# Block 0's last feed-forward quarter as Strassen products in a retention and squared-ReLU kernel

## The chip, the cores and the metric

The kernel runs on one core of a Trainium2 chip. The metric is the device time of one execution in microseconds, as the median of several runs. The names of the engines are those of the profile: PE does matmuls, PEld is PE's loading of weights, DVE is the vector engine, ACT the scalar engine, POOL GpSimd, and SP the queue from which nearly all DMAs are issued.

## The reference, cut to what matters

```python
q, k, v: (8, 8, 576, 64)          # batch, heads, sequence, head size
scores = scale * np.matmul(q, k.transpose(0, 1, 3, 2))
Dmat = np.where(rel >= 0, gamma[:, None, None] ** rel[None, :, :], 0.0)
ret = np.matmul(scores * Dmat[None], v)
x = ret.transpose(0, 2, 1, 3).reshape(4608, 512)
h = np.maximum(x @ w_in, 0.0)     # w_in: (512, 2048)
out = h * h @ w_out               # w_out: (2048, 512)
```

Retention, a causal attention with decay and no softmax, makes x of 4608 tokens by 512. Two feed-forward products follow, with a squared ReLU between them. The weights come in as 64-bit floats and are turned into 32-bit ones by integer operations on the chip.

## The kernel before

**Tiling.** The 4608 tokens are 36 chunks of 128 (`N_CH`) and nine blocks of 512 (`N_BLK`), four chunks to a block. Retention goes chunk by chunk and leaves x of block n, transposed, in a room of SBUF, `xT[n]`. Two rooms alternate, so block n writes over the x of block n - 2. The first feed-forward product of a block is cut into four quarters by `mp`, of 512 of the 2048 columns. It is stored to DRAM as five combinations (`G_KEPT`) of the squared result. When all nine blocks are done, a last stage from line 1141 on takes these back and does the second product as two nested levels of seven Strassen products, with block 0 as the last of `BLOCKS`.

**Two ways of doing a quarter.** Blocks 1 to 8 use `ffn_in` (line 700): seven products of Strassen's scheme (`PRODUCTS`), each of four matmuls with 256 columns at line 717. A 32-bit matmul shows in the profile as two instructions, so a product shows as eight. The three sums a, b and c lie in three PSUM tiles of one pool of three (`ps_f`). DVE adds and squares the results (lines 729 to 743); the fifth product (j = 4, line 736) is read on DVE from the tile of b, into which the seventh (j = 6) accumulates next. The left sides of the products are sums of weights (`sum_w_in`, lines 257 to 260); the right sides are sums of x (`sum_x`, lines 637 to 640), made on DVE. At the start the weights aren't all there yet. Block 0 therefore uses `first_in` (line 667), sixteen plain steps. A step takes one converted weight piece of 128 columns, does four matmuls of 512 columns (line 677, eight instructions), and lets ACT do ReLU and square (lines 683 and 685). The two sums that block 0's store lacks, S1 and S3, are made by `sums_0` (line 1005) in the last stage: DRAM to SBUF, two DVE sums at line 1020, and back, for each of eight slices.

**Conversion of the weights.** A piece of `w_in` is converted by six parts in order, one per call unit of `convert` (lines 227 to 244). The first two are on DVE; `beside` is on ACT (line 235); then come three more on DVE, of which the first doesn't need ACT's result and the second does. Ending a piece triggers the fetch of a later one. `w_out` is converted in the same way, in small parts placed in blocks 1 to 7 by a rate (`late_w2`), and goes to DRAM.

**What sets the order.** Every engine's instructions stand in the order in which this program writes them; there is no planner. The loop at line 915 visits the chunks. A visit, `whole(i - 1)`, does the chunk's matmuls with 64 by 64 weights, in which ACT copies the running state (`grown`, line 501) and x (`x_out`, line 550) and DVE masks the scores (line 491). Then `ffn(i - 1)` runs some feed-forward steps from the list `steps`: three plain ones in block 0, seven products afterwards, so that a block takes four visits. In block 0 each step is preceded by up to four of ACT's copies (`move`), six parts of conversion, and one of two DVE transposes of a later chunk's q and k (`flip`, line 416). The 16 copies per chunk (line 431) distribute what these transposes made. `loads` issues the q, k and v of chunks two or three ahead on SP; POOL scales q (line 396) and v (line 495) as they land.

A guard in `x_out` (line 546) runs leftover steps before x is written over:

```python
while steps and steps[0][0] <= n - 2:
    step()
```

Of the kernel before, what the change touches and what calls it, by code (L numbers as in the profile page):

```python
# [15 lines left out]
C = 128  # L16
CH = C // 2
TOK = 512
# [23 lines left out]
def kernel(  # L42
# [33 lines left out]
    nc = tc.nc  # L76
# [7 lines left out]
    N_DM = d_model // 128  # L84
    N_DF = d_ff // 128
    N_M = N_DF // 2
    N_MP = N_M // 2
    N_MQ = N_M // 2
    N_BLK = n_tok // TOK
    NP = len(PRODUCTS)  # L90
# [34 lines left out]
    G_KEPT = ("A11", "S1", "A12", "S3", "A22")  # L125
# [3 lines left out]
    room = const.tile([128, 15872], F32, name="room")  # L129
# [34 lines left out]
    pieces = [(0, m, e) for m in range(N_M) for e in range(2)]  # L164
    pieces += [(1, mq + mh * N_MQ, e) for mq in range(N_MQ) for mh in range(2) for e in range(2)]
    N_W1 = N_DF
    N_HALF = 1
    stage = [W[5].rearrange("p (o s f) -> p o s f", o=4, s=NP),
             W[6][:, 0:3 * NP * 128].rearrange("p (o s f) -> p o s f", o=3, s=NP)]
# [136 lines left out]
    n_made = [0]  # L306
# [26 lines left out]
    def convert(count):  # L333
        for _ in range(count):
            f = next(w_in_steps, None)
            f and f()
# [32 lines left out]

    st = {i: {} for i in range(N_CH)}  # L370
    u_ps = [None]
    xT = {n: xT_room[1 - n % 2] for n in range(N_BLK)}

# [265 lines left out]

    sums = {}

    def g_of(mp):
        return {name: g_room[mp % 2][:, s, :, :] for s, name in enumerate(G_KEPT)}

    def g_store(n, mp, name):
        nc.sync.dma_start(g_dram[n, G_KEPT.index(name), :, 2 * mp:2 * mp + 2, :], g_of(mp)[name])

    def g_sums(n, mp):  # L650

        g = g_of(mp)
        return [
            lambda: [nc.vector.tensor_tensor(g["S1"], g["S3"], g["A22"], op=ALU.add), g_store(n, mp, "A12")],
            lambda: [nc.vector.tensor_tensor(g["S3"], g["A11"], g["S3"], op=ALU.subtract), g_store(n, mp, "S1")],
            lambda: g_store(n, mp, "S3"),
        ]
# [9 lines left out]
    def first_in(j, halves=(0, 1), at=(0, HT)):  # L667

        assert n_made[0] > j
        wi, m, e = pieces[j]  # L670
        mp, mm = divmod(m, 2)
        p = ps_f.tile([128, 2, HT], F32, tag="f", name="h_ps")
        w = w_in[mp][:, mm, 2 * e:2 * e + 2, :, :].rearrange("p s c f -> p (s c) f")
        lo, hi = halves[0], halves[-1] + 1
        p = p[:, lo:hi, at[0]:at[1]]
        for c in range(N_DM):
            nc.tensor.matmul(p, lhsT=w[:, c, :], rhs=xT[0][:, c, :].rearrange("p (h t) -> p h t", h=2)[:, lo:hi, at[0]:at[1]],  # L677
                             start=(c == 0), stop=(c == N_DM - 1))

        t = g_room[mp % 2][:, 2:5:2, mm, :] if e else g_room[mp % 2][:, 0:4:3, mm, :]  # L680
        t = t[:, lo:hi, at[0]:at[1]]
        some(2)
        nc.scalar.activation(t, p, AF.Relu)
        if hi - lo == 2:
            queue.append(lambda: nc.scalar.activation(t, t, AF.Square))
        else:
            queue.append(lambda: nc.vector.tensor_tensor(t, t, t, op=ALU.mult))
        if mm and e and hi == 2 and at[1] == HT:
            queue.append(lambda: [nc.sync.dma_start(
                g_dram[0, a:b, :, 2 * mp:2 * mp + 2, :].rearrange("s p m t -> p s (m t)"),  # L690
                g_room[mp % 2][:, a:b, :, :].rearrange("p s m t -> p s (m t)")) for a, b in QUARTERS])
        if j >= N_W1 - 4:

            sums_w.setdefault(0, sum_w_in(0)).pop(0)()
            if n_next[0] > 1:
                if 1 not in sums_x:
                    sums_x[1] = sum_x(1)
                sums_x[1].pop(0)()

    def ffn_in(n, mp, j):  # L700

        if j == 0 and mp == 0:

            if n == 1:
                transfers.extend((N_BLK, lambda i=i: fetch_w(i)) for i in range(N_W1, N_W1 + 3))
            if n not in sums_x:
                sums_x[n] = sum_x(n)
            for f in sums_x[n]:
                f()
        left, right, to = PRODUCTS[j]  # L710
        if j in OPENS:
            sums[to] = ps_f.tile([128, 2, HT], F32, tag="f", name=f"h_{to}")
        p = sums[to]
        for mm in range(2):
            w = w_in[mp][:, mm, WI_SLOT[left], :, :]
            for c in range(2):
                nc.tensor.matmul(p[:, mm, :], lhsT=w[:, c, :], rhs=xs[n][right][:, c, :],  # L717
                                 start=(j in OPENS and mm == 0 and c == 0), stop=(j in CLOSES and c == 1),
                                 skip_group_check=True)
        g = g_of(mp)  # L720
        p1, u2, p15 = (p_room[mp % 2][:, s, :, :] for s in range(3))

        def square(t):
            nc.vector.scalar_tensor_tensor(t, t, 0.0, t, op0=ALU.max, op1=ALU.mult)  # L724

        if j == 0:
            nc.scalar.copy(p1, p)
        elif j == 1:
            nc.vector.tensor_tensor(u2, p, p1, op=ALU.add)
        elif j == 2:  # L730
            nc.vector.tensor_tensor(p15, p, p1, op=ALU.add)
        elif j == 3:
            nc.scalar.activation(g["A11"], p, AF.Relu)
        elif j == 4:
            nc.scalar.activation(g["A11"], g["A11"], AF.Square)
            nc.vector.tensor_tensor(g["A22"], p, p15, op=ALU.add)
            square(g["A22"])
        elif j == 5:

            nc.vector.tensor_tensor(g["S3"], p, u2, op=ALU.add)  # L740
            square(g["S3"])
        else:
            nc.vector.tensor_tensor(g["A12"], p, p1, op=ALU.add)
            square(g["A12"])
            queue.extend(g_sums(n, mp))

        if j == 5:
            g_store(n, mp, "A11")
            transfers.append((n, lambda: g_store(n, mp, "A22")))

        if mp == N_MP - 1 and j in (3, 4, 5) and n_next[0] > n + 1:
            if n + 1 not in sums_x:
                sums_x[n + 1] = sum_x(n + 1)
            sums_x[n + 1].pop(0)()
        if j in (6, 0, 1, 2, 3):
            some(2 if n == 1 and mp == 0 else 1)
        if n == 1 and 1 <= j < 5 and mp + 1 < N_MP:
            sums_w.setdefault(mp + 1, sum_w_in(mp + 1)).pop(0)()

        late_w2 = 0.94 * (done[0] - N_0 - 8) - n_w2[0]  # L760
        count = 0 if busy[0] or n == 1 and j == 4 else 2 if late_w2 > 1.5 and j in (0, 3) and n > 1 else late_w2 > 0
        while w_out_next[0] and (count or type(w_out_next[0]) is list):
            f = w_out_next[0]
            if held[0] and type(f) is tuple or ahead[0] <= QUIET and type(f) is list:
                break
            assert n_w2[0] or not [t for t in transfers if t[0] == N_BLK]
            n_w2[0] += 1
            count -= type(f) is not list
            w_out_next[0] = next(w_out_steps, None)
            for f in f if type(f) in (tuple, list) else (f,):  # L770
                f()
            if type(w_out_next[0]) is list:
                break
        if n == N_BLK - 2 and mp == 3 and j in (0, 3):
            assert w_out_next[0] is None
            fetch_w2(j // 3)
# [12 lines left out]
    def block_steps(n):  # L789
        if n == 0:  # L790
            seconds = [(0, first_in, j, (1,), (C, HT)) for j in range(N_HALF)]
            return seconds + [(0, first_in, j) for j in range(N_HALF, N_W1)]
        return [(n, ffn_in, n, mp, j) for mp in range(N_MP) for j in range(NP)]

    QUIET = 2

# [10 lines left out]

    N_0 = N_W1  # L810
    done = [0]

    def ffn(i):

        if steps and steps[0][0] == 0:

            for _ in range((N_W1 - N_EARLY) * C // TOK):
                move(4)
                convert(6)
                for f in flips[:1]:  # L820
                    f()
                del flips[:1]
                step()
            return
        count = N_MP * NP * C // TOK
        while steps and count:
            held[0] = count <= 1

            due = sum(m[0] <= i + 2 for m in moves)
            move(max(2, min(4, -(-due // (count - 1)))) if count > 1 else 0)  # L830
            ahead[0] = count
            busy[0] = len(flips) > 0
            for f in flips[:1]:
                f()
            del flips[:1]
            step()
            count -= 1
        held[0] = busy[0] = False
        ahead[0] = N_DF
# [164 lines left out]

    def sums_0():

        for m in range(N_M):
            t = late1.tile([128, len(G_KEPT), HT], F32, tag="g0", name="g0")

            def move(parts, out):  # L1010
# [213 lines left out]
```

## Time and profile before

| What | us |
|---|---|
| Median of 3 runs | 932.11 (931.95 to 932.25) |
| Profiled execution | 931.9 |
| Its span, first to last instruction | 930.2 |
| First plain step of the last twelve | 43.46 |
| Block 1's first product | 95.12 |
| Last stage, about | 541 to the end |
| DMA over the span | 181.29 MB, mean 195 GB/s |

The profile is of one execution. Times in it count from the first instruction. The span is the time from the first to the last instruction, and the rest of the execution's own time (1.7 us) lies around it. A line of a timeline has the start, the length, the engine, the line of the kernel, the operation and the tiles, and the number of instructions that were merged. A line of waits has the waiting engine and line, then what released it, with the sum in us, the count and the longest. A line of the table by stage has the window, its length, and for PE, PEld, DVE, ACT and POOL the busy time and the number of instructions, then the granted clock, the share of DMA and GB/s.

### The profile page before, as it was taken

What the parts mean: (1) busy time and instruction counts of PE and PEld (TensorE: products, weight loads), DVE (VectorE), ACT (ScalarE), POOL (GpSimd) and SP (SyncE); (2) the same over time, 40 slices, a digit from 0 to 9 for tenths busy, and PEclk for the clock granted to TensorE, in tenths of its full rate; (3) what the DMA queues carried; (4) which work ended last, traced back from release to release, by engine and by line L of the source; (5) the groups of instructions that cost most, each with busy time, mean ns of one, the idle gap of its engine ahead of it and who ended that gap; (6) DMA issues with size and microseconds to landing.
All of it is one profiled execution on the core that took longest, in us unless ns stands there. A gap on an engine that the chain in (4) does not pass through costs nothing.

```text
span 930.2 us, 21072 instructions
## 1 busy us (share of the span) xinstructions
PE 922.4 (99%) x8548; PEld 830.2 (89%) x8548; DVE 755.4 (81%) x1215; ACT 346.2 (37%) x788; POOL 82.9 (9%) x82
## 2 busy tenths in 40 slices
PE   8999999999999999999999999999999999999997
PEld 7654888888888888888888899999999999999997
DVE  5888788888898888979876587888888888877877
ACT  3457767667676676676711110000000000000000
POOL 3222111011111111211000000000000000000000
PEclk9999999999999999999999999999999999999999
DMA  9998657578666775784379996566666575465523
GB/s 226 220 270 218 166 153 202 161 214 267 167 180 184 259 216 146 223 271 137 114 258 355 383 318 193 145 176 191 168 180 183 156 206 155 114 178 142 151 79 68
DMA packets 297376, 181.29 MB, mean 195 GB/s; under 512 B 194368, under 2 KB 270272, under 8 KB 296384
## 3 DMA queue, kind: packets, MB, share of 16 engines
q1 hardware_dynamic: 292208, 178.84, 66.5%
q10 hardware_dynamic: 5072, 1.12, 0.6%
q8 instruction: 67, 1.10, 0.5%
q14 instruction: 29, 0.24, 0.1%
HBM read 109.39 MB, written 70.52 MB: 193 GB/s over the span
## 4 chain that ended last, share of the span: by engine, by line
PE 98%; DVE 1%; DMA 1%; SPq 0%; issue 0%; ACT 0%; DVEq 0%
PE h_b L717 18%; PE o_b L1061 18%; PE h_a L717 12%; PE h_c L717 12%; PE o_c L1061 12%; PE o_a L1061 12%; PE h_ps L677 6%; PE x_ps L574 3%; PE sc_ps L480 2%; PE x_ps L609 1%; PE u_ps L568 1%; DMA q_ld<-in_q_dram 1%; PE sc_ps L509 0%; PE t_ps L445 0%; PE x_ps L535 0%; DVE room L513 0%
## 5 line engine op out<-in xcount | busy, mean ns | idle before, releaser
L717 PE MATMUL h_b<-room,w 128*128 128x256 f32 x768 | 181.4, 379 | 0.0
L431 ACT COPY qk<-flip 32x256 f32<-32x256 f32 x432 | 173.8, 402 | 6.7
L717 PEld LDWEIGHTS h_b<-room,w 128*128 128x128 f32 x768 | 145.9, 190 | 19.8
L717 PE MATMUL h_a<-room,w 128*128 128x256 f32 x512 | 123.9, 385 | 0.0
L717 PE MATMUL h_c<-room,w 128*128 128x256 f32 x512 | 121.0, 379 | 0.0
L717 PEld LDWEIGHTS h_c<-room,w 128*128 128x128 f32 x512 | 97.3, 190 | 13.2
L717 PEld LDWEIGHTS h_a<-room,w 128*128 128x128 f32 x512 | 95.0, 190 | 13.7
L1061 PE MATMUL o_b<-room,w 128*128 128x192 f32 x496 | 90.8, 326 | 0.0
L1074 ACT COPY r<-o_a 128x192 f32<-128x192 f32 x28 | 8.9, 319 | 209.4 <-PE o_a L1061 209.4
L1061 PEld LDWEIGHTS o_b<-room,w 128*128 128x128 f32 x496 | 82.3, 190 | 0.0
L724 DVE SCALAR_TENSOR_TENSOR room<-room 128x512 f32<-128x512 f32 x96 | 66.7, 695 | 3.3
L396 POOL TENSOR_TENSOR q_ld<-q_ld,dv 128x512 f32<-128x512 f32 x34 | 37.7, 1110 | 286.1 <-DMA q_ld<-in_q_dram 257.2
L1061 PE MATMUL o_a<-a,w 128*128 128x192 f32 x352 | 62.6, 326 | 0.0
L1061 PE MATMUL o_c<-room,w 128*128 128x192 f32 x336 | 61.5, 326 | 0.0
L1061 PE MATMUL o_b<-s,w 128*128 128x192 f32 x336 | 61.5, 326 | 0.0
L1061 PE MATMUL o_c<-s,w 128*128 128x192 f32 x336 | 61.5, 326 | 0.0
L677 PE MATMUL h_ps<-room,w 128*128 128x512 f32 (+1 forms) x152 | 57.7, 532 | 0.7 <-DVE w L244 0.6
L1061 PEld LDWEIGHTS o_a<-a,w 128*128 128x128 f32 x352 | 58.1, 190 | 0.1
L1061 PE MATMUL o_a<-room,w 128*128 128x192 f32 x320 | 56.9, 326 | 0.0
L1061 PEld LDWEIGHTS o_c<-room,w 128*128 128x128 f32 x336 | 55.8, 190 | 0.0
L1061 PEld LDWEIGHTS o_b<-s,w 128*128 128x128 f32 x336 | 55.8, 190 | 0.0
L1061 PEld LDWEIGHTS o_c<-s,w 128*128 128x128 f32 x336 | 55.8, 190 | 0.0
(116 smaller groups left out, 1409.2 us busy)
## 6 DMA issues: line engine op xcount, KB each, us to landing
g_dram<-room SPq DMA_DIRECT2D x164, 256.0 KB, 3.8
a<-g_dram SPq DMA_DIRECT2D x30, 512.0 KB, 5.3
room<-g_dram SPq DMA_DIRECT2D x28, 512.0 KB, 5.0
w_dram<-w SPq DMA_DIRECT2D x28, 448.0 KB, 4.5
w<-w_dram SPq DMA_DIRECT2D x7, 1792.0 KB, 9.8
q_ld<-in_q_dram SPq DMA_DIRECT2D x64, 128.0 KB, 4.1
w<-in_moe_w_in_dram SPq DMA_DIRECT2D x16, 512.0 KB, 6.3
w<-in_moe_w_out_dram SPq DMA_DIRECT2D x64, 128.0 KB, 3.4
```

Of the source, the lines that this page charges most:

```text
L396: engine.tensor_tensor(t, t, dv[:, heads, at:at + 1].to_broadcast(list(t.shape)), op=ALU.mult)
L431: nc.scalar.copy(*moves.pop(0)[2:])
L480: nc.tensor.matmul(st[i]["sc"][e][rows(h), hp, :], lhsT=st[i]["kT"][rows(e), hp, t], rhs=st[i]["qT"][rows(e), hp, t], start=True, stop=Tru ...
L568: return [lambda hp=hp, e=e, b=b: nc.tensor.matmul(u[rows(e), hp, :], lhsT=loaded[i][1][rows(h), 2 * hp + e, :], rhs=st[i]["vs"][rows(h), ...
L574: return [lambda hp=hp, e=e, b=b: nc.tensor.matmul(x_at(hp, e, b, h), lhsT=s["vs"][rows(h), head(hp, e), :], rhs=s["ret"][rows(h), e, hp, ...
L609: m = nc.tensor.matmul(x_at(hp, e, b, h), lhsT=u[rows(e), hp, :], rhs=s["qT"][rows(e), hp, CH * h:CH * h + CH], start=clears(b, e), stop=F ...
L677: nc.tensor.matmul(p, lhsT=w[:, c, :], rhs=xT[0][:, c, :].rearrange("p (h t) -> p h t", h=2)[:, lo:hi, at[0]:at[1]], start=(c == 0), stop= ...
L717: nc.tensor.matmul(p[:, mm, :], lhsT=w[:, c, :], rhs=xs[n][right][:, c, :], start=(j in OPENS and mm == 0 and c == 0), stop=(j in CLOSES a ...
L724: nc.vector.scalar_tensor_tensor(t, t, 0.0, t, op0=ALU.max, op1=ALU.mult)
L1061: nc.tensor.matmul(p, lhsT=w_out[j][:, m, WO_SLOT[right], :], rhs=s["lefts"][left][:, m, :], start=(i in OPENS and m == 0), stop=(i in CLO ...
L1074: nc.scalar.copy(r[:, 0, LEFT], p)
```

## The change

Block 0 does only the pieces 0 to 11 as plain steps (`N_PLAIN`), which are its first three quarters. Its last quarter becomes seven products of `ffn_in`, placed after the 28 of block 1 and marked as 2, so that the guard lets them stand until block 4's x is due. Since block 0's x is needed until then, `xT[0]` gets a room of its own, which was unused at that time. The plain steps are dealt out as 1, 2, 2 and 3 to the chunk visits 4 to 7 instead of three each, and both transposes of a chunk are put in the first step. With six parts per step, 14 of 16 pieces are converted in block 0; the parts of the last two are put at fixed places in block 1's first half. The conversion of `w_out` begins seven steps later. The two G rooms alternate by a new rule (`side`), the x sums of block 0 are made before its products and those of block 2 after, and `sums_0` covers six slices instead of eight. The list of steps is longer by seven from block 1 on; as each visit still takes seven, the guard runs seven of them at once in `x_out` of chunk 16.

```diff
+    N_PLAIN = N_W1 - 4
...
-    xT = {n: xT_room[1 - n % 2] for n in range(N_BLK)}
+    xT = {n: xT_room[1 - n % 2] for n in range(1, N_BLK)}
+    xT[0] = room[:, 5120:7168].rearrange("p (c t) -> p c t", c=N_DM)
...
-    def g_of(mp):
-        return {name: g_room[mp % 2][:, s, :, :] for s, name in enumerate(G_KEPT)}
+    def side(n, mp):
+        return (3 + mp if n == 1 else 7 if n == 0 else mp) % 2
+
+    def g_of(n, mp):
+        return {name: g_room[side(n, mp)][:, s, :, :] for s, name in enumerate(G_KEPT)}
...
-        if j >= N_W1 - 4:
+        if j >= N_PLAIN - 4:
...
-        if j == 0 and mp == 0:
+        if j == 0 and (mp == 0 or n == 0):
...
-        if mp == N_MP - 1 and j in (3, 4, 5) and n_next[0] > n + 1:
-            if n + 1 not in sums_x:
-                sums_x[n + 1] = sum_x(n + 1)
-            sums_x[n + 1].pop(0)()
+        after = {1: 0, 0: 2}.get(n, n + 1)
+        if mp == N_MP - 1 and j in (3, 4, 5) and n_next[0] > after:
+            if after not in sums_x:
+                sums_x[after] = sum_x(after)
+            sums_x[after].pop(0)()
...
         if n == 1 and 1 <= j < 5 and mp + 1 < N_MP:
+            assert n_made[0] >= 4 * (mp + 2)
             sums_w.setdefault(mp + 1, sum_w_in(mp + 1)).pop(0)()
-
-        late_w2 = 0.94 * (done[0] - N_0 - 8) - n_w2[0]
+        if n == 1:
+            convert({0: 2, 1: 1, 3: 2, 5: 1}.get(j, 0))
+
+        late_w2 = 0.94 * (done[0] - N_0 - 15) - n_w2[0]
...
-            return seconds + [(0, first_in, j) for j in range(N_HALF, N_W1)]
-        return [(n, ffn_in, n, mp, j) for mp in range(N_MP) for j in range(NP)]
+            return seconds + [(0, first_in, j) for j in range(N_HALF, N_PLAIN)]
+        made_ = [(n, ffn_in, n, mp, j) for mp in range(N_MP) for j in range(NP)]
+        if n == 1:
+            made_ += [(2, ffn_in, 0, N_MP - 1, j) for j in range(NP)]
+        return made_
...
-    N_0 = N_W1
+    N_0 = N_PLAIN
...
-            for _ in range((N_W1 - N_EARLY) * C // TOK):
+            for _ in range({4: 1, 7: 3}.get(i, 2)):
                 move(4)
                 convert(6)
-                for f in flips[:1]:
+                for f in flips:
                     f()
-                del flips[:1]
+                del flips[:]
                 step()
...
-        for m in range(N_M):
+        for m in range(2 * (N_MP - 1)):
             t = late1.tile([128, len(G_KEPT), HT], F32, tag="g0", name="g0")
```

More of the change, by code (lines that the diff above doesn't have):

```diff
@@ L642 @@
     sums = {}
-    def g_of(mp):
-        return {name: g_room[mp % 2][:, s, :, :] for s, name in enumerate(G_KEPT)}
+    def side(n, mp):
+        return (3 + mp if n == 1 else 7 if n == 0 else mp) % 2
+    def g_of(n, mp):
+        return {name: g_room[side(n, mp)][:, s, :, :] for s, name in enumerate(G_KEPT)}
     def g_store(n, mp, name):
-        nc.sync.dma_start(g_dram[n, G_KEPT.index(name), :, 2 * mp:2 * mp + 2, :], g_of(mp)[name])
+        nc.sync.dma_start(g_dram[n, G_KEPT.index(name), :, 2 * mp:2 * mp + 2, :], g_of(n, mp)[name])
     def g_sums(n, mp):
-        g = g_of(mp)
+        g = g_of(n, mp)
         return [
@@ L719, in ffn_in @@
                                  skip_group_check=True)
-        g = g_of(mp)
-        p1, u2, p15 = (p_room[mp % 2][:, s, :, :] for s in range(3))
+        g = g_of(n, mp)
+        p1, u2, p15 = (p_room[side(n, mp)][:, s, :, :] for s in range(3))
         def square(t):
@@ L765, in ffn_in @@
                 break
-            assert n_w2[0] or not [t for t in transfers if t[0] == N_BLK]
+            assert n_made[0] == N_W1 and (n_w2[0] or not [t for t in transfers if t[0] == N_BLK])
             n_w2[0] += 1
```

## The prediction

> **What bounds the kernel now.** I read the page's busy times first, then what PE waited for, then the order of time on PE and DVE around block 0. The page says that the tensor engine is the bound:
>
> ```profile
> span 930.2 us, 21072 instructions
> PE 922.4 (99%) x8548; PEld 830.2 (89%) x8548; DVE 755.4 (81%) x1215; ACT 346.2 (37%) x788; POOL 82.9 (9%) x82
> ```
>
> The share is modelled, so it must be checked against PE's waits. From 15 us to the end there is one:
>
> ```profile
> PE h_ps L677 <- DVE w L244: 0.6, 1, 0.6
> ```
>
> So a microsecond of PE work that goes is a microsecond of time, and any wait that comes is one too. Two views give PE's prices. The timeline of PE in block 1 (start, length, then eight instructions of one product):
>
> ```profile
> 111.31 1.89 PE L717 MATMUL h_b<-room,w 128*128 128x256 f32 x8
> 113.04 1.89 PE L717 MATMUL h_c<-room,w 128*128 128x256 f32 x8
> 114.77 1.89 PE L717 MATMUL h_a<-room,w 128*128 128x256 f32 x8
> ```
>
> From start to start a product takes 1.73 us (113.04 - 111.31); the 1.89 contains an overlap. The timeline of weight loads in a run of three plain steps of block 0 (24 instructions from 43.46):
>
> ```profile
> 44.00 0.19 PEld L677 LDWEIGHTS h_ps<-room,w 128*128 128x128 f32 x1 [0.24 <-issue]
> 53.01 0.19 PEld L677 LDWEIGHTS h_ps<-room,w 128*128 128x128 f32 x1 [0.24 <-issue]
> ```
>
> These are 21 loads apart: 9.01 / 21 = 0.429 us each, so a plain step of eight is 3.43 us, twice a product. Next is the slack of DVE, since the change packs its work closer. The table by stage (PE, PEld, DVE, ACT, POOL busy):
>
> ```profile
> 43.46:95.12 51.66, 51.66 (x628) 27.17 (x624) 43.78 (x69) 33.80 (x67) 12.96 (x11) 1.00 0.94 240
> 95.12:104.06 8.94, 8.94 (x47) 7.90 (x42) 5.76 (x9) 8.35 (x20) 0.31 (x1) 1.00 0.60 153
> ```
>
> The first row is the last twelve plain steps, the second runs from block 1's start to the moment when DVE takes its fifth product (L736 at 104.06). DVE is free for 60.60 - 49.54 = 11.06 us there. Part of that freedom is not for use, as the waits of DVE in the first stretch show:
>
> ```profile
> DVE qk L491 <- PE sc_ps L480: 4.3, 4, 2.1
> DVE w L241 <- ACT w L235: 3.2, 6, 1.1
> ```
>
> The second line is the ping-pong inside a weight conversion: DVE makes the exponent (L227), ACT scales it (L235), DVE needs it again (L241). A conversion on DVE is these five operations, in the groups by line from 44 to 94 us:
>
> ```profile
> L241 DVE SCALAR_TENSOR_TENSOR w<-w,w 128x512 f32<-128x512 f32 x11 | 9.0, 815 | 3.8 <-ACT w L235 3.2
> L238 DVE SCALAR_TENSOR_TENSOR w<-w,w 128x512 f32<-128x512 uint32 x11 | 8.4, 761 | 0.3
> L244 DVE SCALAR_TENSOR_TENSOR w<-w,w 128x512 uint32<-128x512 uint32 x11 | 8.3, 759 | 0.4
> L227 DVE TENSOR_SCALAR w<-w 128x512 uint32<-128x512 uint32 x10 | 4.6, 463 | 0.0
> L231 DVE TENSOR_SCALAR w<-w 128x512 uint32<-128x512 uint32 x10 | 4.2, 420 | 0.0
> ```
>
> Means: 0.815 + 0.761 + 0.759 + 0.463 + 0.420 = 3.22 us a piece.
>
> **What the Trainium skill says.** (1) "Trainium Kernel Development and Optimization", Quick Reference, Reading a trace: matmul busy time is a bad metric of the distance to the limit. This trace agrees in that it shows 99% whether or not PE is well fed, so I use pitches. (2) "PSUM — Partial Sum Buffer", Engine vs sequencer instructions: the queues of ScalarE, VectorE and GpSimdE are strict FIFO, and matmuls start in order. The trace agrees: DVE's conversions, sums and evictions follow the program order, so whatever is queued late delays what stands behind it. (3) "SBUF — State Buffer", Who interferes with whom: a DVE operation with two SBUF inputs and a GpSimd operation that reads SBUF lock each other out. The trace agrees: L238 at 78.11 took 1.44 us instead of 0.69 while a POOL scaling ran from 77.95 to 79.01. The means above contain that.
>
> **The change, part by part.**
>
> PE work. Out go plain steps 12 to 15: 4 x 3.43 = 13.73 us. In come seven products: 7 x 1.726 = 12.08 us (113.04 to 119.95 is four products in 6.91). The number of chunk visits is the same, and the seven that are run at once in `x_out` of chunk 16 adjoin the seven of `ffn(16)`, so no switch is added. Sum: **-1.65 us**.
>
> DVE and ACT work. The four plain steps used ACT for relu and square (0.59 and 0.63 us each, hidden). The products bring eight DVE evictions and squares, two G sums and four x sums, 14 x about 0.61 us (pitch of 736 to 724 and the like) = 8.5 us in a 14.36 us period. Blocks 2 to 8 have the same load in their last quarter and PE keeps its 1.73 pitch there (block 1: 138.21 to 152.5). The two phases after each other, block 1's last quarter and this one, are both of that kind. I cost it at nothing; uncovered, a DVE surplus of 0.5 us at one product.
>
> Late stage. `sums_0` handles 6 slices instead of 8: four fewer of L1020 (0.416 us each) on a DVE that is busy 318.9 of 384 us from 541 to 925, where PE never waits: 0. Fewer SP transfers there, 0. Block 0's last quarter is stored by `g_store` as block 1's is; DMA share is 0.56 around there: 0.
>
> `xT[0]` in its own room: the ACT copy is the same: 0. Block 2's later weight steps (`late_w2` with 15 for 8) begin seven steps later in block 1 and stand where they stood in block 2, since N_0 falls by 4 and seven steps are added: 0.
>
> The packed stretch. This is the cost. PE reaches block 1 earlier by 4 x 3.43 = 13.7 us, and DVE must have done nearly the same work. What DVE no longer has to do before it takes block 1's fifth product: piece 15 (3.22) and the last operation of piece 14 (0.76), together 3.98 us; piece 14's other parts are put by `convert` at j = 0, 1, 3. So DVE has 49.54 - 3.98 = 45.56 us of work in 60.60 - 13.73 = 46.87: 97% full, 1.3 us free where it had 11. What idle time can't be filled: the ACT ping-pong, 3.2 us before and about 2.7 for 9 of 11 pieces; and a wait for the scores at L491, up to 2.0 us in the second chunk (`ffn(5)`: two pieces end about 57, PE brings the scores about 59; it was 2.1 before); together 2.7 to 4.7. DVE then comes 1.4 to 3.4 us late to the fifth product. PE tolerates some of it: the seventh product accumulates into the bank that DVE reads (h_b), one product later: 1.73 - 0.69 - 0.1 = 0.9 us. What is queued behind the late read is j = 5's and j = 6's adds and squares; PE waits for them in turn. Stall: 0.5 to 2.5 us. Lower bound 0, if DVE is late only where PE has slack; a gain is excluded, since PE never waits there now. Upper bound: contention with POOL of 0.75 us hits once or twice more in the packed order, 4 us. ACT has its own form of it: in `ffn(6)` both flips come in the first step, so ACT's chunk copies wait for DVE's transposes, and `grown(7,1)` behind them releases PE's next u matmul; the same for chunk 9's copies before its scores. I get 0 to 1.1 us for each. They don't add: while PE waits early, DVE catches up. I take **+1.5 us** for the whole, the middle of 0.5 and 2.5.
>
> Loads. The stretch is DMA-full (0.94). In each chunk fewer weight fetches precede the next loads, and one G store moves out. v of chunk 7 is scaled by 56.2 (landed 54.9; two fetches, two loads and the like ahead of it are unchanged); PE will need it at 43.46 + 3.6 (one step with its edges) + 2.8 (chunk visit, 53.96 to 56.72) + 7.05 (two steps) + 1.3 (visit's start to its first v of the next chunk, 67.22 to 68.50) = 58.2: slack 2.0 us. Later chunks have 3 us and more. Cost 0; uncovered, 1 to 2 us.
>
> Sum: -1.65 + 1.5 = -0.15. The profiled execution took 931.9 (span 930.2 and 1.7 around it), so 931.75; the median of the runs is 932.11, 0.2 above it: **932.0**.
>
> **The rivals.** *The whole gain*: DVE's and ACT's lateness stays within PE's tolerance. For it: PE is 0.9 us tolerant and the adds before that have two or three products of room. Against: 1.3 us free in 46.9. It gives 932.1 - 1.65 = 930.5. *Slower*: DVE's backlog before block 1, through ACT. The one mechanism: conversions, transposes and ACT's copies in turn make each wait for the other in `ffn(6)` and `ffn(7)`, and DVE is more than 0.9 + 1.65 + 1.9 = 4.4 us late at the fifth product; from 2.5 us late on it is slower than before at all. Price 4 us and more: 932.1 - 1.65 + 4.5 = 935.0. For it: ACT was 9.3 of 10.5 us busy in the last three plain steps, and gets two more conversions there. Against: a stall itself lets DVE catch up. *A load comes late*: chunk 7's v or q, 1 to 2 us besides the 1.5: 933.5. Against it: the loads ahead are fewer. *More than the gain*: nothing in the profile offers PE more than 1.65.
>
> **How the numbers follow.** Forecast 932.0 (931 to 933.2): 0.50. Whole gain 930.5: 0.25. Slower 935.0: 0.15. Late load 933.5: 0.08. Something better: 0.02. A measurement of this kernel can tell about 0.2% from no change, here 1.9 us: 930.2 to 934.0 counts as the same. The whole gain lies just inside it; a fifth of it may fall out (0.05). Faster 0.06, same 0.78, slower 0.16. Range: 930.3 (whole gain) to 934.2, which leaves out most of the slower case.
>
> **What would show it.** Products at a pitch of 1.73 and block 1 starting near 81.4 us (95.12 - 13.7) if nothing waits; PE's waits listing L717 on DVE L736 or room L729, or sc_ps on ACT L431, in sum some 1.5 us; DVE busy about 97% of the stretch from 43 us to block 1's fifth product; the late stage of equal length. Wrong: PE waits of over 3.5 us or none; a wait for POOL v_ld; a pitch over 1.73 in the quarter after block 1 or around chunk 16.

## The result, and the profile after

The changed kernel is slower by 0.4%: 935.6 us as the median of 6 runs (934.55 to 936.2) beside 932.05 us for the kernel before on the same chip (6 runs). The ratio is 1.0038, 95% interval 1.0025 to 1.0051. The profiled execution took 936.2 us, the slowest of the six, with a span of 934.4; before it was 931.9 and 930.2.

The page's first lines, of the kernel after. PE is still the busiest engine at 99%, and the sum of its work as the profile shows it hardly changes, so these lines don't say where 4 us went:

```profile
span 934.4 us, 21125 instructions
PE 922.3 (99%) x8572; PEld 835.3 (89%) x8572; DVE 765.5 (82%) x1225; ACT 343.1 (37%) x783; POOL 82.6 (9%) x82
```

The waits of PE from 15 us on, where the kernel before had one of 0.6 us:

```profile
PE h_b L722 <- DVE room L734: 2.4, 1, 2.4
PE h_ps L682 <- issue: 1.3, 1, 1.3
PE h_b L722 <- DVE room L741: 0.8, 1, 0.8
PE h_ps L682 <- DVE w L245: 0.5, 1, 0.5
PE u_ps L570 <- ACT u_sb L503: 0.5, 1, 0.5
```

L722 is the product matmul (L717 before), L734 the eviction of the second product (L729 before), L741 that of the fifth (L736 before). Block 1's first quarter in the timeline of PE shows the two large ones in their places, before the fifth and the seventh product:

```profile
83.90 1.99 PE L722 MATMUL h_a<-room,w 128*128 128x256 f32 x8
85.73 1.89 PE L722 MATMUL h_b<-room,w 128*128 128x256 f32 x8
87.46 1.89 PE L722 MATMUL h_c<-room,w 128*128 128x256 f32 x8
89.19 1.89 PE L722 MATMUL h_a<-room,w 128*128 128x256 f32 x8
93.45 1.99 PE L722 MATMUL h_b<-room,w 128*128 128x256 f32 x8 [2.38 <-DVE room L734]
95.28 1.89 PE L722 MATMUL h_c<-room,w 128*128 128x256 f32 x8
97.97 1.99 PE L722 MATMUL h_b<-room,w 128*128 128x256 f32 x8 [0.80 <-DVE room L741]
```

Only the packed stretch is longer than it should be. The starts of the runs of weight loads cut it into chunk visits and runs of feed-forward steps; lengths in us:

| | step, then visit of chunk 5 | steps, visit 6 | steps, visit 7 | steps, visit 8 | block 1's first quarter |
|---|---|---|---|---|---|
| lengths that before's runs and visits give | 3.63, 2.77 | 7.06, 2.77 | 7.06, 2.12 | 10.50, 2.01 | 12.28 |
| after | 3.63, 2.77 | 8.60, 3.11 | 7.06, 2.86 | 10.50, 2.03 | 16.00 |

The excess is 1.54 + 0.34 + 0.74 + 0.02 + 3.72 = 6.36 us. PE's listed waits in the stretch make 5.0 of it (2.4 + 1.3 + 0.8 + 0.5; that for L245 lies ahead of it); the rest is lost around them and in gaps too short for the list. From block 1's second quarter to the last stage all is as planned: 445.15 us (101.97 to 547.12) beside 433.07 before (109.48 to 542.55). The difference is 12.08 us, the seven added products to the hundredth. So -13.73 + 12.08 + 6.36 = 4.7. With 0.12 us less before the stretch and 0.37 less in the last stage's end, this is the 4.2 by which the span grew.

The table by stage for that stretch of the kernel after. Its end is where DVE takes the fifth product, as in the prediction's table:

```profile
43.34:83.90 40.56, 38.71 (x596) 21.28 (x593) 32.68 (x53) 25.84 (x55) 10.80 (x10) 1.00 1.00 256
83.90:97.23 13.33, 10.89 (x52) 8.96 (x48) 13.02 (x19) 11.03 (x24) 3.48 (x3) 1.00 1.03 231
```

DVE's work is 32.68 + 13.02 = 45.70 us; 45.56 had been forecast. But it needed 53.89 us for it, not 46.87. Its waits from 43.34 to 97.3:

```profile
DVE w L242 <- ACT w L236: 5.0, 5, 1.8
DVE qk L493 <- PE sc_ps L482: 2.4, 2, 1.9
```

The wait at L493 is 1.95 us in the stretch; the other 0.43 ended just before it. The ping-pong inside the conversions cost 5.0 us for 10 pieces, where it cost 3.2 for 11 before. In the timeline of DVE one sees the four large waits and then the late evictions:

```profile
56.25 0.69 DVE L242 SCALAR_TENSOR_TENSOR w<-w,w 128x512 f32<-128x512 f32 x1 [1.81 <-ACT w L236]
63.32 0.69 DVE L242 SCALAR_TENSOR_TENSOR w<-w,w 128x512 f32<-128x512 f32 x1 [0.88 <-ACT w L236]
69.15 0.69 DVE L242 SCALAR_TENSOR_TENSOR w<-w,w 128x512 f32<-128x512 f32 x1 [0.95 <-ACT w L236]
74.73 0.69 DVE L242 SCALAR_TENSOR_TENSOR w<-w,w 128x512 f32<-128x512 f32 x1 [1.15 <-ACT w L236]
92.75 0.65 DVE L734 TENSOR_TENSOR room<-h_b,room 128x512 f32<-128x512 f32 x1
97.23 0.68 DVE L741 TENSOR_TENSOR room<-h_b,room 128x512 f32<-128x512 f32 x1
```

In the kernel before, the second product's eviction started 2.21 us after that product's first weight load (96.74 to 98.95). Here the load is at 85.52 and the eviction at 92.75, so it is 5.0 us late. The largest wait, 1.81 us, has another origin than the rest. On ACT the exponent (L236, 55.51) stood behind the ReLU of a plain step, and that waited for PE:

```profile
55.01 0.60 ACT L688 ACTIVATE room<-h_ps 128x512 f32<-128x512 f32 x1 [2.90 <-PE h_ps L682]
```

PE was late with this step because of its own gap of 1.3 us. The other four waits make 3.2 us, as much as all six of the kernel before.

### The profile page after: what moved, and what is told of

It reads as the page before. It is cut to its first block, busy times and chain, and to the rows that moved or that the text cites. A ratio compares the mean times of both kernels' runs of the same rounds, so it can differ in the third digit from the quotient of the medians.

```text
span 934.4 us, 21125 instructions
## 1 busy us (share of the span) xinstructions
PE 922.3 (99%) x8572; PEld 835.3 (89%) x8572; DVE 765.5 (82%) x1225; ACT 343.1 (37%) x783; POOL 82.6 (9%) x82
## 4 chain that ended last, share of the span: by engine, by line
PE 96%; DVE 2%; ACT 1%; issue 1%; DMA 0%; SPq 0%; DVEq 0%
PE h_b L722 18%; PE o_b L1073 18%; PE h_a L722 12%; PE h_c L722 12%; PE o_c L1073 12%; PE o_a L1073 12%; PE h_ps L682 4%; PE x_ps L576 3%; PE sc_ps L482 2%; PE x_ps L611 1%; PE u_ps L570 1%; PE idle_ps L857 0%; DMA k_ld<-in_k_dram 0%; PE t_ps L447 0%; PE sc_ps L511 0%
## 5 line engine op out<-in xcount | busy, mean ns | idle before, releaser
L722 PE MATMUL h_b<-room,w 128*128 128x256 f32 x792 | 187.3, 379 | 3.2 <-DVE room L734 2.4
L722 PEld LDWEIGHTS h_b<-room,w 128*128 128x128 f32 x792 | 150.3, 190 | 24.3 <-DVE room L734 2.8
L722 PE MATMUL h_a<-room,w 128*128 128x256 f32 x528 | 127.6, 385 | 0.0
L722 PE MATMUL h_c<-room,w 128*128 128x256 f32 x528 | 124.7, 379 | 0.0
L722 PEld LDWEIGHTS h_c<-room,w 128*128 128x128 f32 x528 | 100.3, 190 | 13.6
L722 PEld LDWEIGHTS h_a<-room,w 128*128 128x128 f32 x528 | 98.0, 190 | 14.1
L729 DVE SCALAR_TENSOR_TENSOR room<-room 128x512 f32<-128x512 f32 x99 | 69.2, 699 | 3.4
L1073 PEld LDWEIGHTS o_a<-room,w 128*128 128x128 f32 x320 | 52.8, 190 | 0.0
```

Of the source, the lines that this page charges most:

```text
L1073: nc.tensor.matmul(p, lhsT=w_out[j][:, m, WO_SLOT[right], :], rhs=s["lefts"][left][:, m, :], start=(i in OPENS and m == 0), stop=(i in CLO ...
```

## The experiments

The theory was called *backlog*. With 13.7 us of PE work gone ahead of block 1, DVE can't do its conversions, transposes and sums in time. It reaches block 1's evictions late, and PE waits for them. The rivals were *supply*, in which the loss begins with PE's own gap of 1.3 to 1.5 us at 52 us; *products*, in which the added products and their run of fourteen cost more than their matmuls; and *flips*, in which putting both transposes in one step costs. All kernels start from the kernel after, but for `before_dve_12`. The kernel before had 932.26 to 932.31 us beside these. The expectations count PE's two waits from weight load to weight load, 2.75 and 1.2 us, where the views above have 2.4 and 0.8, and take the lateness as 5.4.

**DVE's work taken away.** `light_pieces`:

```diff
-            yield from (one, two, beside, three, four)
+            light = j in (12, 13)
+            yield from (None, two, None, None, None) if light else (one, two, beside, three, four)
...
-                five()
+                light or five()
```

> The kernel after, but pieces 12 and 13 are converted by their second part alone (L232, about 0.42 us each on DVE); the other four DVE parts and the ACT part of these two pieces are left out, so a part of block 0's and the later blocks' third and fourth quarters is computed with other weights. DVE has 2 x 2.8 = 5.6 us less to do just ahead of block 1; PE's work and the DMAs are the same. Theory 'backlog' (DVE is 5.4 us late at block 1's second product, L734 at 92.75 us, and PE waits for it 2.75 us and then 1.2 us): both waits go, 931.7 (931.0 to 932.4). Rival 'supply' (the loss begins with PE's own gap of 1.5 us at 52 us, and what follows is its echo): 935 to 936. Rival 'products' (the seven added products and their run of fourteen at chunk 16 cost more than 12.08 us): 935.6.

Measured: 931.82 us (13 runs), ratio 0.9997 (0.9988 to 1.0005). The waits of PE in its profile:

```profile
PE u_ps L571 <- ACT u_sb L504: 0.5, 1, 0.5
PE h_ps L683 <- DVE w L245: 0.4, 1, 0.4
PE u_ps L571 <- issue: 0.3, 1, 0.3
PE t_ps L448 <- DMA k_ld<-in_k_dram: 0.2, 1, 0.2
```

No product waits for DVE any more; block 1's first quarter takes 12.28 us. The products and the run of fourteen are all still there, so *products* falls. What these two pieces ask of DVE, and of ACT with it, costs 3.8 us of the median. In the same way `light_six` lightens the pieces 8 to 13:

```diff
+            light = 8 <= j <= 13
```

> As light_pieces, but for the pieces 8 to 13: each of these six is converted by its second part alone, and the other four DVE parts and the ACT part are left out, so weights of three quarters are wrong. DVE has 16.8 us less to do between 50 us and block 1. Theory 'backlog plus loads' (the DVE backlog costs 3.7 us at block 1 and about 1.1 at the visits of chunks 6 and 7; what is left, 0.4 to 1.5 us between 47 and 58 us, is PE waiting for a load or its own instructions and has nothing to do with DVE): 930.6 to 931.6, with the loss between 47 and 58 us still there. If DVE and ACT were all: 930.4, and every stretch at its length from the kernel before.

Measured: 931.76 us (21 runs, 930.21 to 935.2), ratio 0.9993 (0.9987 to 1.0). Slightly over the range, and as expected the rest of the loss stayed between 47 and 58 us: the visit of chunk 5 took 4.05 us instead of 2.77. But here it isn't free of DVE and ACT. PE waited 0.75 us for ACT's copy of the state, which stood behind an exponent that DVE had begun late (47.05), and only 0.2 for a q that POOL got at 49.71 us and not at 47.5.

**The waiting inside a conversion.** `no_exponent`:

```diff
-            yield from (one, two, beside, three, four)
+            yield from (one, two, beside if j < 7 else None, three, four)
```

> The kernel after, but the ACT part of the conversion (L236) is left out for the pieces from 7 on, so these weights have a wrong exponent. DVE's own work is the same; it no longer waits for ACT inside a conversion (5.0 us of its idle time from 43 to 97 us), and ACT has nine operations of 0.63 us less. Theory 'backlog', in the form that the idle time in the ping-pong is what DVE couldn't fill: DVE comes 1 to 2 us late to block 1 instead of 5.4, PE waits some 0.5 to 1 us there, 932.0 to 933.0. If the sheer amount of DVE work decides and not the waiting for ACT: 934.5 to 935.6. Rival 'supply': 935 to 936.

Measured: 934.44 us (12 runs), ratio 1.0026 (1.0017 to 1.0034). That is 1.2 us off the kernel after, less than the 2.6 to 3.6 expected, and at the edge of what the expectation gives for the amount of work alone (934.5). In its profile PE waits 1.2 us for L734 and 0.7 for L741, and the first quarter takes 14.77 us. The two readings aren't parted by it, though, since DVE came early to its next wait and stood there:

```profile
59.77 0.69 DVE L493 TENSOR_TENSOR qk<-sc_ps,msk 128x512 f32<-128x512 f32 x1 [3.87 <-PE sc_ps L482]
```

From the first plain step to the fifth product its idle time fell only from 8.2 to 6.4 us. Taking away one wait of a strict queue moved most of the idle time to the next.

**DVE's work moved to PE.** `turn_11` and `turn_10` turn two chunks or one by PE instead of by DVE's transposes and ACT's copies:

```diff
-    N_TURN = 9
+    N_TURN = 11
```

> The kernel after with chunks 9 and 10 turned on PE as chunks 4 to 8 are (N_TURN 11 for 9): DVE does four transposes less (4 x 0.62 = 2.5 us) and ACT 32 copies of 0.41 us less, 13 us, with four copies of 0.55 us more; PE does two turns more, 2 x 0.64 = 1.3 us. Theory 'backlog': PE's waits at block 1's fifth and seventh product (3.9 us) and at the visit of chunk 7 (0.7) go, 935.6 - 4.6 + 1.3 = 932.3 (931.5 to 933). Rival 'supply': 936.9, since PE only gets more to do. Rival 'products': 936.9.

> The kernel after with chunk 9 alone turned on PE (0.64 us more on PE, 1.25 us less on DVE and 6.6 us of copies less on ACT, all in ffn(6) and ffn(7)). Theory 'backlog': the visit of chunk 7 no longer waits (0.7 us), DVE is 2.5 to 3.5 us late at block 1 instead of 5.4, so of the 3.7 us there 1 to 2 are left: 935.6 - 0.7 - 2.2 + 0.64 = 933.3 (932.7 to 934.2). If ACT's copies play no part and only DVE's 1.25 us count: 934.5 to 935.5.

Measured: 934.07 us for `turn_11` (21 runs, 932.55 to 935.75; 1.0018, 1.0012 to 1.0025) and 934.15 for `turn_10` (14 runs; 1.0017, 1.0010 to 1.0025). So `turn_11` missed its range of 931.5 to 933. Its profiled execution is its fastest, 932.55, and agrees with the theory: no wait of PE above 0.3 us, and the stretch is 52.09 us long, 0.6 above the sum. The median is 1.5 us more, and no trace shows where. `turn_10` meets its expectation at the upper end; in its profile the visit of chunk 7 no longer waits and 2.0 us are left in the first quarter, but the visit of chunk 6 lost 1.2.

**A piece converted later, in a kernel that computes everything.** `defer_13`:

```diff
-                convert(6)
+                convert(0 if done[0] == N_PLAIN - 1 else 6)
...
-        if n == 1 and 1 <= j < 5 and mp + 1 < N_MP:
+        lo = 3 if mp == 2 else 1
+        if n == 1 and lo <= j < lo + 4 and mp + 1 < N_MP:
...
-            convert({0: 2, 1: 1, 3: 2, 5: 1}.get(j, 0))
+            convert(({0: 2, 1: 2, 2: 2} if mp == 2 else {0: 2, 1: 1, 3: 2, 5: 1}).get(j, 0))
...
-        late_w2 = 0.94 * (done[0] - N_0 - 15) - n_w2[0]
+        late_w2 = 0.98 * (done[0] - N_0 - 22) - n_w2[0]
```

> The kernel after, but piece 13 isn't converted in the last plain step: pieces 13, 14 and 15 are converted in the first, second and third quarter of block 1, the sums of the last quarter's weights move from j = 1 to 4 of the third quarter to j = 3 to 6, and the conversion of w_out begins seven steps later at a slightly higher rate. DVE has 3.2 us less ahead of block 1. Theory 'backlog': at block 1's second product DVE is 2 us late instead of 5.4, within the 2.8 us that PE tolerates there, so the wait of 2.75 us goes and that of 1.2 us at the seventh product may stay: 932.0 to 933.0. If DVE's lateness isn't the cause: 935.6.

> defer_13 with chunk 9 turned on PE (0.64 us more on PE, 1.25 us less on DVE, 16 copies of 0.41 us less on ACT). Theory 'backlog': both waits of block 1's first quarter go, and the wait at the visit of chunk 7 for ACT's copy: 932.05 - 1.65 + 0.64 = 931.0, plus 0.4 to 1.5 us lost between 47 and 58 us: 931.4 to 932.5. If turning adds load waits as in turn_11's slower executions: 933 to 934.

Measured: 933.26 us for `defer_13` (13 runs; 1.0009, 1.0001 to 1.0017), 2.3 less than the kernel after and slightly over the range. As expected the wait at the fifth product is gone and that at the seventh is left:

```profile
PE h_b L722 <- DVE room L741: 1.0, 1, 1.0
PE h_ps L682 <- DVE w L245: 0.7, 1, 0.7
PE u_ps L570 <- ACT u_sb L503: 0.5, 1, 0.5
```

With chunk 9 turned on PE as well: 932.44 us (13 runs; 1.0000, 0.9992 to 1.0008). All its waits on DVE in block 1 are gone, the first quarter is at 12.28. It gives the change's loss back and is no faster than the kernel before. Of PE's 1.65 us the turn takes 0.64; the profiled execution (931.4) loses 0.35 between 47 and 58 us and keeps the rest. The median is 1.0 us above that execution, and no trace shows where. Of the twelve kernels none that computes everything beat the kernel before.

**The kernel before, with more work for DVE.** `before_dve_12`:

```diff
+    idle_room = room[:, 5120:5632]
+    nc.gpsimd.memset(idle_room, 1.0)
...
                 convert(6)
+                nc.vector.tensor_tensor(idle_room, idle_room, idle_room, op=ALU.mult)
                 for f in flips[:1]:
```

> The kernel before with one DVE operation more (128x512 on an unused room, about 0.65 us) in each of the last twelve plain steps, 7.8 us in all; outputs are not touched. PE, loads and visits keep the pace of before, so only DVE's load changes. Theory 'backlog': of the 11 us of DVE's idle time in that stretch only some 4 to 6 can be used, so PE waits at block 1's second and fifth to seventh products, 933.0 to 935.0. If the early visits, loads or the order of the flips are what costs and DVE's 11 us are free: 932.1.

Measured: 935.34 us (7 runs), ratio 1.0027 (1.0016 to 1.0038), 3.0 us more. The size is slightly over the range; the place is another. Its first quarter of block 1 is at 12.28 us, and PE waits in the visits of chunks 5 and 7, which take 4.18 and 3.10 us:

```profile
PE u_ps L570 <- ACT u_sb L503: 1.9, 2, 1.2
```

L503 is the copy of the state, queued on ACT behind the exponent of a piece that DVE hasn't begun. So the kernel before had little room on DVE by itself, with its own visits and loads, though 11 us looked free. And once PE has waited there, DVE has caught up.

**Order and place.** `flips_apart` puts the two transposes back in two steps, `deal_2123` deals the plain steps as 2, 1, 2, 3, `turn_11_deal` does that with `turn_11`, and `ahead_3` fetches raw pieces later:

```diff
-                for f in flips:
+                for f in flips[:1]:
...
-            for _ in range({4: 1, 7: 3}.get(i, 2)):
+            for _ in range({4: 2, 5: 1, 7: 3}.get(i, 2)):
...
-    N_AHEAD = 4
+    N_AHEAD = 3
```

> The kernel after with the two transposes of a chunk in two steps, as in the kernel before. Theory 'backlog': DVE's work is the same and only its order changes, so block 1's waits stay, 935 to 936; ACT doesn't wait 0.9 us for the transposes in the second step of ffn(6), so the 0.7 us at the visit of chunk 7 may go, but four copies come later and chunk 9's scores may wait for them. Rival 'flips' (putting both transposes in one step is what costs): 932 to 933.

> The kernel after with the plain steps dealt out as 2, 1, 2, 3 instead of 1, 2, 2, 3, so the visit of chunk 5 begins 3.4 us later and all later visits when they did. Theory 'loads' for the stretch from 47 to 58 us (chunk 7's k and q and the weight fetches come as fast as the DMA engines bring them, and PE is there too early): PE's loss in that stretch, 1.9 us in the profile of after, falls to 0.3 or less, and DVE, which idled 1.8 us behind it, is less late at block 1, 932.5 to 934. If the loss there is of the instruction stream and not of the early visit: 935 to 936.

> Chunks 9 and 10 turned on PE, as in turn_11, and the plain steps dealt as 2, 1, 2, 3. Theory 'backlog plus loads': both losses go and the two turns cost 1.3 us, 932.05 - 1.65 + 1.3 + 0.3 = 932.0 (931.5 to 932.6), with a smaller spread than turn_11's 3.2 us. If the early visit isn't the cause of turn_11's slower executions: 934 as turn_11.

> The kernel after with raw weight pieces fetched three ahead of the conversion instead of four, so from about 44 us on each fetch of 512 KB stands one piece further back in SP's queue, behind loads of q, k and v. Theory 'loads' (the DMA engines are full from 43 to 84 us and what PE needs waits behind fetches that aren't needed yet): PE's loss from 47 to 58 us falls, 933.5 to 935. If conversion then waits for its raw piece, DVE gets later: 936 or more. If DMA order plays no part: 935.6.

Measured: 938.06 us (5 runs; 1.0064, 1.0051 to 1.0076), 939.07 (5 runs; 1.0064, 1.0050 to 1.0078), 934.7 (21 runs; 1.0027, 1.0020 to 1.0033) and 935.95 (6 runs; 1.0035, 1.0023 to 1.0047). *Flips* falls as the main cause: apart they are worse. The 0.7 us at the visit of chunk 7 did go (2.12 us), but four copies come too late for chunk 9's scores, and PE stands for 4.2 us, so that the kernel lies above its range too:

```profile
PE sc_ps L482 <- ACT qk L433: 4.2, 2, 3.9
PE u_ps L570 <- ACT u_sb L503: 0.7, 1, 0.7
```

After that no product of block 1 waits for DVE. `deal_2123` and `ahead_3` were misses. The loss from 47 to 58 us went as expected (runs and visits within 0.2 us), and so it did in `ahead_3`, yet neither got faster. In `deal_2123` the visit of chunk 7 took 4.58 us, 2.2 of them waiting for ACT's copy, and block 1's quarter 16.13; in `ahead_3` it is 3.17 and 16.31. `turn_11_deal` missed too: two products wait 1.1 us in all for DVE, and the quarter takes 13.90. So *supply* is real, but it isn't what delays block 1: without it the quarter takes as long as with it. In `deal_2123` and `ahead_3` a part of that time is half clock, as the last section shows.

## Why the prediction was wrong, point by point

**PE's work: right.** The added products cost 12.08 us, and the plain steps that are left keep their pitch, so that 13.73 went with the others; nothing else of the change's parts (products' evictions, the run of fourteen at chunk 16, the room, `sums_0`, the later `w_out`) shows in the trace from 101.97 us on. The choice of pitches over busy time was right as well: PE's busy time is 922.4 and 922.3 us in executions that lie 4.3 us apart, which the trace of before alone couldn't show. (The sentence of the Trainium skill on it stands under Performance Expectations, just ahead of the Quick Reference that the prediction names.)

**The step that failed is the stall of the packed stretch.** It was named with its mechanism, its place and its engines, bounded at 0 to 4 us, and taken at +1.5. It measured 4.5 us in the profiled execution: 3.72 in block 1's first quarter and 0.74 at the visit of chunk 7. DVE's amount of work was right (45.56 forecast, 45.70 measured). The idle time that can't be filled was not: 2.7 to 4.7 us in the forecast, 53.89 - 45.70 = 8.2 in the trace. The ping-pong with ACT made 5.0 of it and not 2.7, since I scaled it by the number of pieces. It depends on what stands ahead of the exponent on ACT. Behind the turned chunk's copies (63.32) and the chunk copies (69.15, 74.73) it waited as in the kernel before, where they stand in its way too; the 1.81 us behind the late ReLU are new, and PE lost 1.54 us there itself. The wait for the scores was 1.95, as forecast. The remaining 1.2 us are gaps too short for the list, which the forecast left out, though the kernel before has 1.3 of them in the same span. So DVE took the fifth product 7.0 us after the planned time and not 1.4 to 3.4, and 4.4 us later after block 1's actual start than before (13.33 us for 8.94).

**Taking the middle was the second error.** The working gave 0.5 to 2.5 us from lateness alone, and then added the visits (0 to 1.1 us each) under "they don't add". That rule holds where one early wait covers the whole backlog, as in `flips_apart` and `before_dve_12`. In the kernel after the early wait for ACT was 0.74 us and the late ones 3.7.

**A late supply was costed at nothing.** This is a second term that failed: 0 in the forecast, 1.54 + 0.34 = 1.9 us in the trace. It isn't chunk 7's v or q. The profile shows a gap of PE that nothing it records explains:

```profile
53.85 0.30 PEld L682 LDWEIGHTS h_ps<-room,w 128*128 128x128 f32 x2 [2.10 <-issue]
```

The kernels that deal the steps in the same way and wait for nothing else there lost 0.1 to 1.9 us between 47 and 61 us. In all eight of them the gap stands at the same place of the program, between the sixth and the seventh weight load of one plain step, where no new data is needed. And it ends with the same thing, a packet of 16 KB in one of the profile's queues of the kind "instruction":

```profile
q8 instruction: 67, 1.10, 0.5%
```

The packet ends between 51.21 and 52.29 us, and PE goes on 1.4 to 1.6 us after that end (in the kernel after 53.85 after 52.29). The 0.34 us at the visit of chunk 6 have the same sign, 60.43 after 58.99. PE's 17,144 matmuls and weight loads over 67 packets make 256 to a packet, so this queue looks like PE's own instructions. That they came late is the likely cause, read off the traces; no run moved that fetch alone. The DMA share rose from 0.94 to 1.00 in the stretch.

**The rivals.** The slower rival had the right mechanism and the right size: its stall of 4.5 us is what the trace shows. The rival of a late load had the right size, 1 to 2 us, but named another cause. The forecast held them to exclude each other, and both came in one execution: -1.65 + 4.5 + 1.9 = 4.7. That 935.0 lies near the measured 935.6 is in part luck, then. The slower rival was given 0.15. Its weight should have come from the table: DVE 97% full, in a queue that stops at every wait on ACT, isn't a likely place to lose only 1.5 us.

## What to carry to other kernels

When work is taken off the bounding engine in a stretch, compute how full the next engine becomes there. In these profiles DVE's work as a share of the planned time (46.87 us, and 0.64 for each chunk turned on PE) parts them well: at 0.85 (`light_pieces`) and 0.87 (`defer_13_turn_10`) no product of block 1 waited for it, at 0.90 none in `turn_11` and two in `turn_11_deal`, and from 0.92 (`defer_13`) on PE always waited for DVE or ACT. At 97% the time was 7 us too short. These figures are of one stretch with one mix of waits. Each strict queue that waits for another inside the stretch adds idle time that depends on what else stands in that other queue. To keep the gain, the second engine's work must leave the stretch first; moving one piece's conversion and one chunk's turn was just enough to break even.

## What the runs showed of the hardware

A short wait of PE can cost more than itself. In `flips_apart` half clock began near the end of the wait of 3.9 us and lasted 6.8 us (84.9 to 91.7). The table by stage, whose last columns are the granted clock, the DMA share and GB/s:

```profile
82.00:86.00 4.00, 0.16 (x2) 0.17 (x2) 3.83 (x5) 2.72 (x6) 2.37 (x2) 0.86 1.04 246
86.00:90.00 4.00, 3.64 (x93) 3.25 (x94) 2.47 (x5) 1.08 (x3) 1.96 (x2) 0.50 0.75 168
90.00:94.00 4.00, 4.00 (x16) 3.38 (x15) 2.43 (x5) 3.00 (x8) 0.59 (x1) 0.78 0.01 2
```

In `ahead_3` and `deal_2123` waits of 2.08 and 1.89 us at block 1's fifth product had the same result, 3.4 us at half clock, so that this product took 3.2 us; in the kernel after a wait of 2.38 us at the same place had not. The `ahead_3` timeline:

```profile
92.30 3.18 PE L722 MATMUL h_b<-room,w 128*128 128x256 f32 x8 [2.08 <-DVE room L734]
95.28 2.43 PE L722 MATMUL h_c<-room,w 128*128 128x256 f32 x8
```

The Trainium skill, "TensorE: Matmul & The Clock Gate", What's actually happening, describes this: the clock falls to half after an idle window of about 3.4 us, and the window runs free. The half clock, the length of 3.4 us and the free window agree; the idle time that sufficed was shorter here, 1.9 us by the profile. The traces show when it does. In all fourteen the clock changes only at whole multiples of 3.413 us after it first rose, at 4.1 to 7.2 us (26 of them from 4.21 to 92.95 in `ahead_3`). Cut into such windows, half clock follows each window in which PE stood idle for 1.89 us or more, and none with 1.68 or less, about half a window. In `ahead_3` the whole wait lay in one window (89.54 to 92.95). In the kernel after the longer one was split by the edge at 92.57, 1.50 and 0.88 us, and nothing followed. So it matters where in a window a wait falls.

That may be a part of why the packed kernels spread by 1.5 to 5 us from run to run where the kernel before spreads by 1.4 to 1.8. The mean clock of each execution fits in some: in `light_six` the two at 935.2 us have 0.998 and the other nineteen, up to 932.4, 0.999 or 1.0, and in `deal_2123` the three at 939.1 us and more have 0.995 or 0.996 and the two faster ones 0.997 and 0.999. In the kernel after there is no such order.
